# U's large loads ahead of its single rows, and the sine part of batch 0 ahead of the cosine part on TensorE

## The chip, the cores and the metric

The kernel runs on one core of a Trainium2 chip. The metric is the time of one execution on the device, in microseconds. The core's engines each work through their own queue in order: TensorE (PE, with its weight loads listed as PEld), VectorE (DVE), ScalarE (ACT), GpSimd (POOL) and SyncE (SP, which issues transfers only). Semaphores tie the queues together. SP and ACT can ask for transfers on a hardware queue, POOL on a software queue; all of them are served by the same 16 DMA engines.

## The reference

```python
X = np.fft.fft(x, axis=1)          # x: 8 x 3136 x 256
X = np.fft.fft(X, axis=2)
x = X.real
h = x.transpose(0, 2, 1) @ U @ V   # U: 3136 x 32, V: 32 x 3136
u = x + h.transpose(0, 2, 1)
out = u + np.maximum(u @ w_ch1, 0) @ w_ch2   # 256 -> 1024 -> 256
```

A Fourier transform over the sequence and over the channels (only the real part is kept), a low-rank mixing along the sequence, and a two-layer perceptron over the channels, with residual sums.

## The kernel before

The sequence transform is written as matrix products with tables of sines and cosines. These tables are made on the chip at the start: `phase` (L229) reduces the angle on DVE, `sine` (L235) and `cosine` (L241) apply the sine function on ACT (`cosine` takes an absolute value first, then a sine, with a tile `ab` between). `tabs[0]` holds sines, `tabs[1]` cosines, each with eight rows `i` of 393 columns and 32 further columns. Symmetries of the tables save work: `odd_row` makes a sine row in full, the other sine rows are made in half and mirrored (`mirror_even`), and most cosine rows are copies of sine rows, turned or with the sign changed (`cosine_odd`, `cosine_low`, `cosine_high`), spread over ACT, POOL and DVE.

The input is folded before it meets the tables. The sequence of a batch is cut into four quarters of 98 partitions with eight elements each, and one partition more for single rows; a "forward" quarter is added to or taken from a "reversed" one. U is folded so too, by `fold_u` (L262): sixteen float32 matmuls on PE with flip matrices `fl` and `nfl` (made by POOL and, in `signs`, L253, by DVE). `UR` holds U reversed, `UF` forward; each comes in one large load of 196 KB (L143) and one load of a single row (`load_0r`, L94 and `load_0f`, L88). `lower_u` copies one half of the result out of PSUM on ACT and `join_u` makes sum and difference on DVE.

Batch 0 has its own path, for it must be ready first. Four large loads (`first_r`, `first_f` for `a` = 0 and 1) and one load of the single rows (`first_0`) bring it into `xb` as bf16, on POOL's queue. `fold_pe(typ, t, a, first)` (L797) folds one quarter with four matmuls of 512 columns: `typ` 0 is the part that meets the sine table, 1 the part for the cosine table; `t` is 1 for the reversed load, 0 for the forward one; `a` is the half of the sequence. `M[typ, a]` are the PSUM tiles that it fills. `keep_m` copies M of `a` = 0 out of PSUM; `half_m` (L820) then makes the half sums and differences on DVE into `G[0]`, the stationary operand of `seq` (L437), the sequence transform.

The folded U is transformed by `transform_u` (L293) in four steps, `us[0]` to `us[3]` for sines and `uc` for cosines: `contract` (sixteen matmuls, L303), `keep` (ACT, L309), `turn` (eight matmuls, L316), and `evict` (ACT, L321 and L322), which fills the tables' 32 further columns. A value `hv` per partition halves some table rows (`halve`, L326) and is used in `evict`.

PE's clock is kept up with filler matmuls (`busy`, L170) whose results nobody reads.

Up to L964 the order of the program is the order on each engine (a manual schedule). After the start a loop over 49 chunks of 512 rows runs the perceptron on PE, with the folds and transforms of batches 1 to 7 spread between its steps by a table of due slots. Loads of later batches are issued by POOL when their buffers come free; SP issues the transposed copies of `u`, the output and the loads of single columns (L499, L508).

Of the kernel before, what the change touches and what calls it, by code (L numbers as in the profile page):

```python
# [8 lines left out]
TWO_PI = 2.0 * math.pi  # L9
HALF_PI = 0.5 * math.pi  # L10
BF16 = mybir.dt.bfloat16
FP32 = mybir.dt.float32
I32 = mybir.dt.int32
AL = mybir.AluOpType
AF = mybir.ActivationFunctionType
# [3 lines left out]
KP = PQ + 1  # L19
NI = 8  # L20
NQ = 393
# [6 lines left out]
def kernel(  # L28
# [9 lines left out]
    nc = tc.nc  # L38
    B, S, D = x.shape
    R = moe_U.shape[1]  # L40
# [9 lines left out]
    gen = setup.enter_context(tc.tile_pool(name="gen", bufs=2))  # L50
# [8 lines left out]
    def rev(t, b, a, w):  # L59

        return bass.AP(t.tensor, t.offset + (b * S + S - 784 - a * HALF) * w,
                       [[8 * w, PQ], [1, 8 * w]])
# [10 lines left out]
    def first_f(a):  # L73
        gather(xb[:PQ, a, 0].rearrange("p i d -> p (i d)"), x, S // 8 - 1,
               xidx[:PQ, 0, a:a + 1], 8 * D, D)

    def first_r(a):
        nc.gpsimd.dma_start(out=xb[:PQ, a, 1].rearrange("p i d -> p (i d)"), in_=rev(x, 0, a, D))

    def first_0():  # L80
        nc.gpsimd.dma_start(out=xb[PQ:KP].rearrange("p a t i d -> p a (t i) d"),
                            in_=bass.AP(x.tensor, x.offset,
                                        [[D, 1], [HALF * D, 2], [0, 2 * NI], [1, D]]))
# [4 lines left out]
    def load_0f(t, dst_f, b, w, q):  # L88
        lo = t.offset + b * S * w
        q.dma_start(out=dst_f[PQ:KP],  # L90
                    in_=bass.AP(t.tensor, lo + (NI - 1) * w,
                                [[w, 1], [HALF * w, 2], [-w, NI], [1, w]]))

    def load_0r(t, dst_r, b, w, q):  # L94
        lo = t.offset + b * S * w
        q.dma_start(out=dst_r[PQ:KP].rearrange("p a i d -> p a (i d)"),
                    in_=bass.AP(t.tensor, lo, [[w, 1], [HALF * w, 2], [1, NI * w]]))
# [17 lines left out]
    def const(v):  # L115
        t = cpool.tile([P, 1], FP32, name=f"c{len(consts)}", tag=f"c{len(consts)}")
        nc.vector.memset(t, v)
        consts.append(t)
        return t

    consts = []
    c_pi, c_npi, c_nhp = const(math.pi), const(-math.pi), const(-HALF_PI)
    c_half = {b: const(-float(2 ** (b - 1))) for b in (15, 17)}
    UF = gen.tile([KP, 2, NI, R], FP32, tag="uf", name="uf", bufs=1)
    UR = gen.tile([KP, 2, NI, R], FP32, tag="ur", name="ur", bufs=1)
    xidx = cpool.tile([P, B, 2], I32, name="xidx")
    krow = gen.tile([P, 2, NQ], FP32, tag="krow", name="krow", bufs=1)
    ncol = cpool.tile([P, NI], FP32, name="ncol")
# [8 lines left out]
    lrow = gen.tile([P, 2, P], FP32, tag="lrow", name="lrow", bufs=1)  # L137
    pcol = gen.tile([P, 1], FP32, tag="pcol", name="pcol", bufs=1)
    QD = P // 2
    load_0r(moe_U, UR, 0, R, nc.sync)  # L140
    load_0f(moe_U, UF, 0, R, nc.sync)
    for t, n0, step in ((UR, S - 784, -HALF), (UF, 1, HALF)):
        nc.sync.dma_start(out=t[:PQ].rearrange("p a i d -> p a (i d)"),  # L143
                          in_=bass.AP(moe_U.tensor, moe_U.offset + n0 * R,
                                      [[8 * R, PQ], [step * R, 2], [1, 8 * R]]))
    first_r(0)
    first_f(0)
    first_0()
    nc.gpsimd.iota(fl[:, 0], pattern=[[1, P]], base=-(PQ - 1), channel_multiplier=1,
                   allow_small_or_imprecise_dtypes=True)  # L150
    nc.gpsimd.iota(fl[:, 1], pattern=[[1, P]], base=0, channel_multiplier=-1,
# [18 lines left out]
    def busy(n, a=None):  # L170

        idle = psum.tile([P, 512], FP32, tag="p2", name="idle", bufs=2)
        for _ in range(n):
            if a is None:
                nc.tensor.matmul(idle[:, :256], ones[:, :P], ones[:], start=True, stop=True)
            else:
                nc.tensor.matmul(idle[:, :NQ], a[:PQ, 0, 0, :P], a[:PQ, 0, 0, :NQ],
                                 start=True, stop=True)

    busy(26)  # L180
    for t in (EOF_, EOR_):
        nc.vector.memset(t.rearrange("p a i d -> p (a i) d")[:, :, 257:258], 0.0)
    G = [[cpool.tile([KP, NI, GW], BF16, name=f"g{s}{par}", tag=f"g{s}{par}") for par in range(2)]
# [7 lines left out]
    def va_zeros(s):  # L191
# [6 lines left out]
    tabs = [cpool.tile([KP, NI, 2, QW], BF16, name="tabs", tag="tabs"),  # L198
            cpool.tile([KP, NI, 2, QW], BF16, name="tabc", tag="tabc")]
# [41 lines left out]
    def cosine(out_, y, bits):  # L241
        pp = y.shape[0]
        ab = gen.tile(list(y.shape), FP32, tag="ab", name="ab", bufs=1)
        nc.scalar.activation(ab[:], y, AF.Abs, bias=c_half[bits][:pp])
        nc.scalar.activation(out_, ab[:], AF.Sin, scale=TWO_PI / 2 ** bits, bias=c_nhp[:pp])

    NH = NQ // 2 + 1
    flip = cpool.tile([P, 2, P], BF16, name="flip")
    nid = gen.tile([P, P], BF16, name="nid", bufs=1)
    phe = gen.tile([KP, NI // 2, 2, NH], I32, name="phe", bufs=1)  # L250
    GU = gen.tile([KP, 2, 2, NI, R], BF16, tag="gu", name="gu", bufs=1)

    def signs():  # L253

        nc.vector.tensor_scalar(nfl[:], fl[:], 0.0, -1.0, op0=AL.is_equal, op1=AL.mult)
        nc.vector.tensor_single_scalar(fl[:], fl[:], 0.0, op=AL.is_equal)
        for t in (fl, nfl):
            nc.vector.tensor_copy(t[:KP, 0, PQ:KP], t[:KP, 1, PQ:KP])
        nc.scalar.copy(flip[:], fl[:])
        nc.scalar.copy(nid[:], nfl[:, 1])  # L260
# [19 lines left out]
    def join_u(ur):  # L280

        for typ, op in ((0, AL.subtract), (1, AL.add)):
            nc.vector.tensor_tensor(GU[:, typ], pf[0][:], ur[:], op=op)

    hv = cpool.tile([P, 1], FP32, name="hv")
    hw = cpool.tile([P, 1], FP32, name="hw")
# [43 lines left out]
    def cells(t, i, col, step, n, skew):  # L330

        v = tabs[t][:, i, :, :]
        return bass.AP(v.tensor, v.offset + col, [v.ap[0], [QW + skew, 2], [step, n]])

    def turned_copy(dst, src, sgn):

        if sgn > 0:
            nc.gpsimd.tensor_copy(dst, src)
        else:
            nc.scalar.activation(dst, src, AF.Copy, scale=-1.0)  # L340

    def mirror_even(t, i):

        odd_m = (i + 1) // 2 % 2 == 1
        dst, src = cells(t, i, 0, 1, NH - 1, 1), cells(t, i, NQ - 1, -1, NH - 1, 0)
        if i == 1:
            nc.scalar.copy(dst, src)
        else:
            turned_copy(dst, src, 1 if odd_m == (t == 0) else -1)

    def cosine_odd(i):

        dst, src = cells(1, i, 1, 1, NQ - 1, 0), cells(0, i, NQ - 2, -1, NQ - 1, 1)
        if i == 4:
            nc.gpsimd.tensor_copy(dst, src)
        else:
            nc.scalar.activation(dst, src, AF.Copy, scale=1.0 if i == 0 else -1.0)

    def cosine_low(i):

        dst, src = cells(1, i, NH - 1, 1, NH, 1), cells(0, i, NQ - 1, -1, NH, 0)
        if i == 1:
            nc.gpsimd.tensor_copy(dst, src)
        else:
            nc.vector.tensor_single_scalar(dst, src, -1.0, op=AL.mult)
# [385 lines left out]
    def odd_row(i):  # L751
        pho = gen.tile([KP, 2, NQ], I32, tag="pho", name="pho")
        phase(pho[:], krow[:KP], ncol[:KP, i:i + 1], 15)
        sine(tabs[0][:, i, :, :NQ], pho[:], 15, 1)
# [3 lines left out]
    cosine_odd(2)  # L758
    odd_row(4)
    signs()  # L760
    nc.vector.tensor_scalar(hv[:], ncol[:, NI - 1:NI], 0.0, -0.5, op0=AL.is_equal, op1=AL.mult)
    nc.vector.tensor_scalar(hw[:], ncol[:, NI - 1:NI], 0.249, -0.5, op0=AL.is_gt, op1=AL.mult)
    nc.vector.scalar_tensor_tensor(hv[:], hv[:], 1.0, hw[:], op0=AL.add, op1=AL.add)
    odd_row(6)
    pf = fold_u()
    busy(2)
    for m, i in enumerate((7, 5, 3, 1)):
# [9 lines left out]
        if i == 3:  # L777
            mirror_even(0, 3)
    join_u(ur)
    mirror_even(0, 1)  # L780
    cosine_low(1)
    cosine_odd(4)
# [9 lines left out]
    def gathered(typ, a, tags):  # L792

        M[typ, a] = [psum.tile([KP, 4, P], FP32, tag=t, name="m", bufs=2 if t == "p2" else 3)
                     for t in tags]

    def fold_pe(typ, t, a, first):  # L797

        for n in range(2):
            v = xb[:, a, t, 7 - 4 * n if t else 4 * n, :]  # L800
            for m, w in enumerate((-1, 1)):
                nc.tensor.matmul(M[typ, a][n][:],  # L802
                                 nid[:KP, :KP] if typ == 0 and (t + m) % 2 else flip[:KP, 1, :KP],
                                 bass.AP(v.tensor, v.offset + P, [v.ap[0], [-D if t else D, 4],
                                                                  [w, P]]),
                                 start=first and m == 0, stop=not first and m == 1)
# [34 lines left out]

    gathered(0, 0, ("p1", "p1"))
    gathered(1, 0, ("p1", "p2"))
    for t in (1, 0):
        for typ in range(2):
            fold_pe(typ, t, 0, t == 1)
    gathered(0, 1, ("p2", "dft"))
    fold_pe(0, 1, 1, True)
    cosine(tabs[1][:, 7, :, NH - 1:NQ], phe[:, 0], 15)
    us[0]()  # L850
# [1 line left out]
    for a in range(2):  # L852
        load_second(a)
    us[1]()
    cosine_odd(0)
    fold_pe(0, 0, 1, False)
    us[2]()
    for n in range(2):
        keep_m(0, n)
    phase(pd[:], lrow.rearrange("p a l -> p (a l)"), pcol[:], 17)  # L860
    gathered(1, 1, ("p1", "p1"))
    fold_pe(1, 1, 1, True)
    busy(3, tabs[0])
    for n in range(2):
        half_m(0, 0, n)
    us[3]()
# [1 line left out]
        half_m(0, 1, n)  # L868
    nc.vector.tensor_copy(cells(1, 7, 0, 1, NH - 1, 1), cells(1, 7, NQ - 1, -1, NH - 1, 0))
    halve(1)  # L870
    cosine(tabs[1][:, 3, :, NH - 1:NQ], phe[:, 2], 15)
    nc.scalar.copy(cells(1, 3, 0, 1, NH - 1, 1), cells(1, 3, NQ - 1, -1, NH - 1, 0))
    cosine_low(5)
    cosine_high(1)
# [131 lines left out]
```

## Time and profile before

| what | value |
|---|---|
| runs, median of 3 | 458.23 us (457.78 to 458.64) |
| the profiled execution, whole time | 459.67 us |
| its span, first to last instruction | 457.9 us |
| PE busy in the span | 445.5 us |
| ACT busy | 293.3 us |
| DVE busy | 348.6 us |
| mean granted PE clock | 0.992 |
| moved by DMA | 65.38 MB, mean 143 GB/s |

A row of the timeline gives the start in us from the span's start, the duration (of a merged group: from its first start to its last end), engine, line, operation, tiles as out<-in, shape, count, and in brackets how long the engine was idle before and what ended that. A matmul's own row is longer than its share of PE, because matmuls are pipelined; the distance between the starts of two neighbours is what one costs. A row of the chain of waits gives start, duration and what the chain went through.

### The profile page before, as it was taken

What the parts mean: (1) busy time and instruction counts of PE and PEld (TensorE: products, weight loads), DVE (VectorE), ACT (ScalarE), POOL (GpSimd) and SP (SyncE); (2) the same over time, 40 slices, a digit from 0 to 9 for tenths busy, and PEclk for the clock granted to TensorE, in tenths of its full rate; (3) what the DMA queues carried; (4) which work ended last, traced back from release to release, by engine and by line L of the source; (5) the groups of instructions that cost most, each with busy time, mean ns of one, the idle gap of its engine ahead of it and who ended that gap; (6) DMA issues with size and microseconds to landing.
All of it is one profiled execution on the core that took longest, in us unless ns stands there. A gap on an engine that the chain in (4) does not pass through costs nothing.

```text
span 457.9 us, 8080 instructions
## 1 busy us (share of the span) xinstructions
PE 445.5 (97%) x2991; PEld 323.1 (71%) x3044; DVE 348.6 (76%) x813; ACT 293.3 (64%) x563; POOL 63.2 (14%) x115
## 2 busy tenths in 40 slices
PE   7999999999999999999999999999999999999996
PEld 4555766666777777777777777777777777777775
DVE  8488999969897869977997779877898666443433
ACT  7476745756865577655865586656865586655562
POOL 8824212200012002100102002200000000000000
PEclk9799999999999999999999999999999999999999
DMA  6993997994378636683378527792253333334343
GB/s 133 219 225 62 174 204 165 157 205 112 114 214 210 138 89 158 195 220 109 84 219 201 146 73 191 208 209 71 69 111 97 93 97 88 94 115 108 102 129 103
DMA packets 103238, 65.38 MB, mean 143 GB/s; under 512 B 73794, under 2 KB 99612, under 8 KB 100452
## 3 DMA queue, kind: packets, MB, share of 16 engines
q1 hardware_dynamic: 97534, 39.10, 37.4%
q0 software_dynamic: 5664, 25.75, 20.9%
q8 instruction: 24, 0.39, 0.3%
q14 instruction: 16, 0.13, 0.1%
HBM read 29.33 MB, written 25.69 MB: 120 GB/s over the span
## 4 chain that ended last, share of the span: by engine, by line
PE 85%; DVE 7%; DMA 3%; issue 2%; SPq 1%; ACT 1%; POOL 0%; DVEq 0%; ACTq 0%
PE p L707 35%; PE p L691 32%; PE pt L452 5%; PE ph L665 4%; PE pth L428 2%; DMA uf<-in_moe_U_dram 2%; DMA cr<-in_x_dram 1%; PE m L802 1%; DVE eor L386 1%; PE pst L604 1%; PE pst L613 1%; SPq L508 1%; PE pf L268 1%; DVE eof L386 1%; DVE u L681 1%
## 5 line engine op out<-in xcount | busy, mean ns | idle before, releaser
L693 ACT ACTIVATE h<-p 128x512 bf16<-128x512 f32 x392 | 223.6, 598 | 129.5 <-PE p L691 116.9
L691 PE MATMUL p<-u,w 128*128 128x512 bf16 x734 | 208.6, 379 | 2.2 <-DVE u L681 0.5
L707 PE MATMUL p<-w,h 128*128 128x256 bf16 x1568 | 204.2, 273 | 1.3
L707 PEld LDWEIGHTS <-h 128*128 128x128 bf16 x1568 | 153.0, 98 | 51.4 <-DVE o L716 0.8
L691 PEld LDWEIGHTS <-w 128*128 128x128 bf16 x784 | 105.9, 144 | 35.5 <-issue 1.7
L713 DVE TENSOR_TENSOR o<-p,ut 128x4 f32<-128x4 f32 (+1 forms) x100 | 16.4, 164 | 56.8 <-PE p L707 54.4
L55 POOL DMA_INDIRECT xf<-in_x_dram,xidx x14 | 17.9, 1276 | 184.3 <-DVE eof L386 172.9
L716 DVE TENSOR_TENSOR o<-p,ut 128x254 f32<-128x254 f32 (+1 forms) x100 | 40.9, 409 | 0.0
L715 DVE TENSOR_TENSOR o<-p,ut 128x254 f32<-128x254 f32 (+1 forms) x100 | 40.8, 408 | 0.0
L681 DVE TENSOR_TENSOR u<-ph,S 128x512 bf16<-128x512 f32 (+23 forms) x63 | 34.5, 557 | 0.0
L681 DVE TENSOR_TENSOR u<-ph,T 128x512 bf16<-128x512 f32 (+23 forms) x63 | 34.4, 557 | 0.0
L386 DVE TENSOR_TENSOR eor<-xr 99x1024 bf16<-99x1024 f32 x28 | 34.1, 1220 | 0.1
L386 DVE TENSOR_TENSOR eof<-xf 99x1024 bf16<-99x1024 f32 x28 | 33.7, 1220 | 0.0
L665 PE MATMUL ph<-va,ta 128*128 128x512 bf16 (+15 forms) x124 | 28.6, 328 | 0.1
L452 PEld LDWEIGHTS <-g 98*128 98x128 bf16 (+1 forms) x152 | 14.6, 98 | 13.0 <-issue 0.7
L459 DVE TENSOR_TENSOR tab<-pt,ev 128x32 bf16<-128x32 f32 x32 | 6.1, 191 | 16.8 <-PE pt L452 16.0
L395 DVE TENSOR_TENSOR eos<-eof,eor 99x1024 bf16<-99x1024 bf16 (+1 forms) x28 | 18.8, 687 | 0.0
L615 DVE TENSOR_TENSOR S<-evd,pst 128x392 bf16<-128x392 f32 (+1 forms) x24 | 13.6, 566 | 6.5 <-PE pst L613 6.1
L452 PE MATMUL pt<-tabs,g 98*128 98x425 bf16 x80 | 17.7, 344 | 0.0
L399 DVE TENSOR_TENSOR g<-eos 99x2048 bf16<-99x2048 bf16 (+1 forms) x14 | 17.0, 1220 | 0.0
L452 PE MATMUL pt<-tabc,g 98*128 98x425 bf16 x72 | 15.5, 344 | 0.0
L665 PEld LDWEIGHTS <-ta 128*128 128x128 bf16 (+1 forms) x128 | 11.9, 98 | 3.1 <-ACT ta L636 0.6
(188 smaller groups left out, 363.2 us busy)
## 6 DMA issues: line engine op xcount, KB each, us to landing
out_dram<-o SPq DMA_DIRECT2D x48, 512.0 KB
xr<-in_x_dram POOLq DMA_DIRECT2D x14, 784.0 KB, 7.0
xb<-in_x_dram POOLq DMA_DIRECT2D x2, 392.0 KB, 7.6
ut<-u SPq DMA_TRANSPOSE x49
w<-in_moe_w_ch_dram POOLq DMA_DIRECT2D x1, 512.0 KB, 8.4
out_dram<-o SPq DMA_DIRECT2D x4, 128.0 KB
va<-in_moe_V_dram POOLq DMA_DIRECT2D x2, 196.0 KB, 5.8
w<-in_moe_w_ch_dram POOLq DMA_DIRECT2D x1, 256.0 KB, 6.7
```

The source lines that it names most:

```text
L55: nc.gpsimd.indirect_dma_start(out_, None, bass.AP(t.tensor, t.offset, [[w, rows], [1, w]]), bass.IndirectOffsetOnAxis(idx, 0), element_of ...
L386: pin(nc.vector.tensor_tensor(dst[:, a, :, part * P:(part + 1) * P].rearrange("p i (k t) -> p i k t", k=2), lo, hi, op=AL.subtract if part ...
L395: pin(nc.vector.tensor_tensor(EOS[:, a, :, cols], EOF_[:, a, :, cols], EOR_[:, a, ::-1][:, :, cols], op=op))
L399: pin(nc.vector.tensor_tensor(G[b % 2][par][:, :, cols], EOS[:, 0, :, cols], EOS[:, 1, :, cols], op=AL.add if par == 0 else AL.subtract))
L452: nc.tensor.matmul(pt[:], g[:kp(i), i, P * typ:P * (typ + 1)], tabs[typ][:kp(i), i, par, :], start=(n == 0), stop=(n == NI // 2 - 1))
L665: nc.tensor.matmul(ph, TA[b % 2][:k, s * P:(s + 1) * P], VA[b % 2][:k, lo:hi], start=start, stop=True)
L681: nc.vector.tensor_tensor(u[:, s, col:col + hi - lo], ph[:, col:col + hi - lo], src, op=AL.add)
L691: nc.tensor.matmul(p1[:], W1[:, s, j::JT], k["u"][:, s, :], start=(s == 0), stop=(s == 1))
L693: LAST[0] = nc.scalar.activation(k["h"][:, j, :], p1[:], AF.Relu)
L707: nc.tensor.matmul(p2[:, t % w, :], h[:, j, rs], W2[:, j, :], start=(j == 0), stop=(j == JT - 1))
L715: nc.vector.tensor_tensor(o[:, ts, 1:P], p2[:, :w, 1:P], ut[:, ts, 1:P], op=AL.add)
L716: nc.vector.tensor_tensor(o[:, ts, P + 1:D], p2[:, :w, P + 1:D], ut[:, tT, P - 1:0:-1], op=AL.add)
```

## The change

```diff
-    load_0r(moe_U, UR, 0, R, nc.sync)
-    load_0f(moe_U, UF, 0, R, nc.sync)
+    load_0f(moe_U, UF, 0, R, nc.scalar)
     for t, n0, step in ((UR, S - 784, -HALF), (UF, 1, HALF)):
         nc.sync.dma_start(out=t[:PQ].rearrange("p a i d -> p a (i d)"),
                           in_=bass.AP(moe_U.tensor, moe_U.offset + n0 * R,
                                       [[8 * R, PQ], [step * R, 2], [1, 8 * R]]))
+    load_0r(moe_U, UR, 0, R, nc.sync)
+    first_0()
     first_r(0)
     first_f(0)
-    first_0()
...
-    busy(26)
+    busy(27)
...
     signs()
-    nc.vector.tensor_scalar(hv[:], ncol[:, NI - 1:NI], 0.0, -0.5, op0=AL.is_equal, op1=AL.mult)
-    nc.vector.tensor_scalar(hw[:], ncol[:, NI - 1:NI], 0.249, -0.5, op0=AL.is_gt, op1=AL.mult)
-    nc.vector.scalar_tensor_tensor(hv[:], hv[:], 1.0, hw[:], op0=AL.add, op1=AL.add)
+    cosine_odd(0)
     odd_row(6)
...
     join_u(ur)
+    nc.vector.tensor_scalar(hv[:], ncol[:, NI - 1:NI], 0.0, -0.5, op0=AL.is_equal, op1=AL.mult)
+    nc.vector.tensor_scalar(hw[:], ncol[:, NI - 1:NI], 0.249, -0.5, op0=AL.is_gt, op1=AL.mult)
+    nc.vector.scalar_tensor_tensor(hv[:], hv[:], 1.0, hw[:], op0=AL.add, op1=AL.add)
...
-    for t in (1, 0):
-        for typ in range(2):
-            fold_pe(typ, t, 0, t == 1)
     gathered(0, 1, ("p2", "dft"))
+    fold_pe(0, 1, 0, True)
+    fold_pe(0, 0, 0, False)
+    fold_pe(1, 1, 0, True)
     fold_pe(0, 1, 1, True)
...
-    cosine_odd(0)
     fold_pe(0, 0, 1, False)
     us[2]()
+    fold_pe(1, 0, 0, False)
+    ab3 = gen.tile([KP, 2 * NH], FP32, tag="ab3", name="ab3", bufs=1)
+    nc.scalar.activation(ab3[:], phe[:, 2].rearrange("p a k -> p (a k)"), AF.Abs,
+                         bias=c_half[15][:KP])
...
-    busy(3, tabs[0])
+    busy(2, tabs[0])
...
-    cosine(tabs[1][:, 3, :, NH - 1:NQ], phe[:, 2], 15)
+    nc.scalar.activation(tabs[1][:, 3, :, NH - 1:NQ], ab3.rearrange("p (a k) -> p a k", a=2),
+                         AF.Sin, scale=TWO_PI / 2 ** 15, bias=c_nhp[:KP])
```

U's single row for `UF` is now asked for by ACT's queue, the two large loads of U come first on SP's, and `UR`'s single row last of the three. On POOL `first_0` is issued ahead of batch 0's large loads. Three small instructions for `hv` move behind `join_u` on DVE. `cosine_odd(0)` moves up on ACT to stand ahead of the fourth sine row. On PE the sine quarters of batch 0 come ahead of the cosine quarters: of the four quarters of `a` = 0 the last cosine one is put behind U's turn. The cosine of table row 3 is made in two places: the absolute value earlier, the sine where the whole was. One filler matmul is added at the start and one taken away later. What is computed stays the same.

## The prediction

> **What bounds the kernel now.** I read the page first, then the chain of waits over the first 26 us, the busy time by stretches of the clock, the timelines of the engines, and the DMA queues.
>
> ```profile
> PE 445.5 (97%) x2991; PEld 323.1 (71%) x3044; DVE 348.6 (76%) x813; ACT 293.3 (64%) x563; POOL 63.2 (14%) x115
> ```
>
> TensorE is busy in 97% of the span (page, part 1), so time is won only where it stands idle or runs at half clock; both happen in the first 17 us, where the diff works. The chain of waits there, with start, duration, and what it is:
>
> ```profile
> 2.78 8.10 DMA uf<-in_moe_U_dram
> 10.88 0.14 issue
> 11.01 3.71 PE pf L268 x8
> ...
> 21.87 1.89 DVE g L822 x3
> ```
>
> The start hangs on U: its second large load is asked for at 2.78 and lands at 10.88, then TensorE folds U (L268), folds batch 0 (L802), and waits for VectorE's first three half sums (L822). The stretches of the clock (columns: busy time of PE, PEld, DVE, ACT, POOL, granted clock, DMA share, GB/s):
>
> ```profile
> 6.65:10.06 3.41, 1.76 (x9) 1.22 (x8) 3.27 (x11) 2.28 (x5) 3.11 (x7) 1.00 1.00 225
> 10.06:13.48 3.42, 3.24 (x9) 1.84 (x8) 1.70 (x5) 3.39 (x8) 3.11 (x7) 0.50 1.00 193
> 13.48:16.89 3.41, 3.41 (x10) 1.89 (x10) 1.83 (x6) 1.78 (x5) 2.99 (x6) 0.50 1.08 202
> 98.81:102.22 3.41, 2.60 (x18) 1.91 (x18) 2.18 (x5) 1.87 (x5) 0.00 (x0) 1.00 1.26 94
> ```
>
> A stretch of 3.41 us in which PE was busy 1.76 us (52%) was followed by two at half clock; one at 2.60 us (76%) kept the clock. So the wait for U costs twice: idle time, and then half speed from 10.06 to 16.89. PE's timeline gives the prices:
>
> ```profile
> 1.35 5.58 PE L175 MATMUL idle<-ones 128*128 128x256 bf16 x26 [1.35 <-DVE ones L169]
> 8.57 1.51 PE L268 MATMUL pf<-ur,fl 99*99 99x256 f32 x6 [1.65 <-DMA ur<-in_moe_U_dram]
> 9.92 0.91 PE L268 MATMUL pf<-ur,nfl 99*99 99x256 f32 x2
> ...
> 20.34 0.85 PE L303 MATMUL pu<-tabs,gu 98*32 98x393 bf16 x16
> 21.13 0.42 PE L802 MATMUL m<-xb,flip 99*99 99x512 bf16 x1
> ...
> 22.04 0.83 PE L316 MATMUL put<-sel,wu 128*98 128x64 bf16 x8
> 22.70 1.05 PE L802 MATMUL m<-xb,flip 99*99 99x512 bf16 x4
> 23.81 0.67 PE L177 MATMUL idle<-tabs 98*128 98x393 bf16 x3
> 24.32 0.89 PE L452 MATMUL pt<-tabs,g 98*128 98x425 bf16 x4
> ```
>
> At full clock six matmuls of the U fold take 9.92 - 8.57 = 1.35, 0.225 each; at half clock 3.71 / 8 = 0.46. Four of batch 0's fold take 22.04 - 21.13 = 0.91, 0.23 each at full clock. The sine contraction of U (L303) takes 0.79, its turn (L316) 22.70 - 22.04 = 0.66, one wide filler (L177) (24.32 - 23.81) / 3 = 0.17.
>
> **U's loads.** SyncE's timeline, and the hardware DMA queue in the answer for 6 to 8 us (packets, MB, share of 16 engines):
>
> ```profile
> 0.75 0.80 SPq L96 DMA_DIRECT2D ur<-in_moe_U_dram  x1
> 1.61 0.65 SPq L90 DMA_DIRECT2D uf<-in_moe_U_dram  x1
> 2.31 0.43 SPq L143 DMA_DIRECT2D ur<-in_moe_U_dram  x1
> ```
>
> ```profile
> q1 hardware_dynamic: 321, 0.31, 48.2%
> ```
>
> The two large loads are 0.39 MB, and 0.31 MB of this queue moves only between 6 and 8 us, when batch 0's first large load has passed. Now the large loads go first, at 0.75 and about 1.6, 1.5 and 1.2 us earlier than at 2.31 and 2.78, while POOL issues the small row (L81) ahead, and so asks for the first large load of batch 0 later, by the 0.4 to 0.8 that such an issue takes in SP's rows. What U lands at isn't shown by this trace: the bounds are 8.57, as now, and 0.75 + 0.80 + 1.3 = 2.9 (its first issue, and 0.196 MB at 0.31 MB in 2 us). I take "before 6.9", since both are asked for before any of batch 0's bulk is on the engines. UR's single row now stands last of the three on SP, behind 2 x 196 KB, and the first matmul needs it; UF's goes from ACT's queue. That issue on ACT is not in the trace; SP's rows bound it at 0.4 to 0.8. ACT has cover for it:
>
> ```profile
> 3.18 0.95 ACT L238 ACTIVATE tabs<-pho,c 99x786 bf16<-99x786 int32 x1 [1.15 <-DVE pho L233]
> ...
> 5.46 0.86 ACT L357 ACTIVATE tabc<-tabs 99x784 bf16<-99x784 bf16 x1
> ...
> 8.79 0.95 ACT L238 ACTIVATE tabs<-pho,c 99x786 bf16<-99x786 int32 x1 [1.13 <-DVE pho L233]
> ...
> 14.06 0.52 ACT L347 COPY tabs<-tabs 99x392 bf16<-99x392 bf16 x1
> 16.15 0.62 ACT L244 ACTIVATE ab<-phe,c 99x394 f32<-99x394 int32 x1 [1.57 <-DVE gu L283]
> 16.81 0.62 ACT L245 ACTIVATE tabc<-ab,c 99x394 bf16<-99x394 f32 x1
> 21.32 0.49 ACT L309 CAST wu<-pu 128x393 bf16<-128x393 f32 x1 [3.89 <-PE pu L303]
> ```
>
> It idled 1.15 us before its first sine, so I take 0; without cover it costs up to 0.8 on ACT's chain.
>
> **U's fold.** With U there, it starts when the flip matrices are ready and the fillers end:
>
> ```profile
> 6.63 0.15 DVE L258 COPY nfl<-nfl 99x1 f32<-99x1 f32 x1
> 6.70 0.15 DVE L761 TENSOR_SCALAR hv<-ncol 128x1 f32<-128x1 f32 x1
> ```
>
> The matrices are ready at 6.78; 26 fillers end at 6.93, 27 at about 7.0 (0.1 for one more, since the clock is full by then). So the fold runs from 7.0, with no hole: stretch 6.65 to 10.06 is then over 95% busy and the clock stays. 16 x 0.225 = 3.60, to 10.60; two fillers 0.22, to 10.82; four quarters of batch 0 in 16 x 0.23 = 3.64, to 14.46.
>
> **ACT and DVE around it.** The three hv instructions leave DVE's path ahead of the fourth sine row: that is about 0.3 earlier (8.5 in place of 8.79). cosine_odd(0), 0.86 at L357, goes into ACT's gap, which shrinks to about 0.85: nothing. ACT's last table copy then ends at 14.58 - 0.3 = 14.28, just ahead of PE's 14.46. Next on ACT come Abs, Sin and the eviction: 14.28 + 0.62 + 0.62 + 0.49 = 16.0. The hv instructions come back behind U's join on DVE, which has waited there for PE until now: nothing. The Abs of table row 3 is only moved, into a gap on ACT.
>
> **The new order on PE.** L303 from 14.46 to 15.25; sine quarter of the other half 0.91, to 16.16; turn 0.66 (its input is there at 16.0), to 16.82; eight matmuls of the cosine part 1.82, to 18.64; two fillers 0.34, to 18.98. VectorE's three half sums, 1.89 from 16.2, end at 18.1 and are covered. The first real transform matmul, at 24.32 now, then starts at 18.98: 5.3 us earlier.
>
> **What the quarters need.** The last one of the sine part comes from POOL's fourth large load:
>
> ```profile
> 6.74 1.01 POOL L55 DMA_INDIRECT xb<-in_x_dram,xidx  x1 [0.30 <-issue]
> ```
>
> ```profile
> DMA to landing us min/median/max: 7.5/8.0/8.8
> ```
>
> The second fence is from the answer on the tile xb. The load lands at 6.74 + 8.8 = 15.5 at the latest; PE now wants it at 15.25. POOL's issue time does not change (three instructions change places), and the engines have U's 0.39 MB out of the way earlier. So 0 to 0.3 is lost; up to 1.1 if the first load's 0.8 carries through. I take 0.
>
> Behind 24 us I take it that all work follows PE; the one load of which the chain says otherwise is rival (3). So 459.67 - 5.3 = 454.4 for the profiled execution (the span and what lies around it); that execution stands 1.44 above the median, so 458.23 - 5.3 = **452.9** on the scale of the runs. Its own range: 452.2 to 453.8.
>
> **Rivals.** (1) **The clock drops anyway.** The stretch 10.06 to 13.48 was 95% busy, mostly with float32 matmuls, and did not bring the clock back; so these may not count. Then it drops at 10.06: 2.4 matmuls of U left at 0.46, fillers 0.44, four of batch 0's fold at 0.46 to 13.48, the other twelve at 0.23: 16.2 in place of 14.46, a gain of 3.6, so 454.6; 456.4 if it stays low until 16.89. Against it: the same rows also fit a threshold between 95 and 100%. [...]
>
> (2) **U lands no earlier**, because UR's row waits behind the large loads and batch 0's bulk: PE starts at 8.57 as now, the clock falls, and only the new order gains: L303 four matmuls earlier, at 20.34 - 0.91 = 19.43, then 0.79, 0.91, 0.66, 1.82 and 0.34 as above, to 23.95 in place of 24.32: 0.4, so 457.8. For it: 0.31 MB of U moved only once batch 0's first load had passed. Against it: the engines are empty when U is asked for.
>
> (3) **The gain is given back at the column loads.**
>
> ```profile
> 94.95 6.87 DMA cr<-in_x_dram
> ```
>
> This load ends a wait at 101.8, and the DMA engines are full there (share 1.26 in the stretch from 98.81); if it lands no earlier, all 5.3 are lost: 458.2. Against it: its queue's first issue follows the compute, so it moves too.
>
> (4) **Slower: the quarters come late and the clock falls again.** If the load above landed after 16.9, PE would idle over 1.65 us in the stretch 13.48 to 16.89, and drop to half clock for two stretches (3.4 lost) and a third one while it waits for evictions (1.7): 1.7 + 3.4 + 1.7 = 6.8, so 1.5 slower, 459.7. It needs the load to be 1.4 later than the latest landing above.
>
> **Numbers.** Forecast 0.66, rival (1) 0.17, (2) 0.07, (3) 0.05, (4) 0.05. A measurement can tell about 0.2%, 0.9 us: faster 0.83, same 0.12, slower 0.05. The range goes from 451.9 (own low end and 0.3 for a shorter fold) to 456.5 (both ends of rival (1)).
>
> **What would show it.** Right: L268 from about 7.0 with no DMA wait, granted clock 1.00 from 6.65 on, L303 near 14.5, the first L452 near 19, cr landing near 96.5. Wrong: a second stretch at 0.50, a DMA wait ahead of L268 or of a quarter, or an ACT chain that ends later than 14.6.

## The result, and the profile after

| | before | changed |
|---|---|---|
| median | 458.23 us (457.08 to 460.0, 7 runs) | 454.88 us (454.4 to 461.75, 7 runs) |
| ratio to before | | 0.9923, 95% interval 0.9902 to 0.9943 |
| profiled execution, span | 457.9 us | 453.4 us |
| mean granted clock in it | 0.992 | 0.999 |

By the medians the change makes the kernel 3.35 us faster; the ratio of the runs gives 0.77%. A few runs fall into a second, slower state (here the one at 461.75 us, at a granted clock of 0.992); the ratios, and the 74 runs of the kernel before that are sorted below, leave these out. The forecast was 452.9, a gain of 5.3; the measured time lies inside the stated range, towards its slow side.

TensorE's timeline of the changed kernel (its fold of batch 0 is now line 803):

```profile
1.35 4.96 PE L175 MATMUL idle<-ones 128*128 128x256 bf16 x27 [1.35 <-DVE ones L169]
6.55 1.51 PE L268 MATMUL pf<-ur,fl 99*99 99x256 f32 x6 [0.24 <-issue]
7.90 0.59 PE L268 MATMUL pf<-ur,nfl 99*99 99x256 f32 x2
8.33 1.46 PE L268 MATMUL pf<-uf,fl 99*99 99x256 f32 x6
...
13.46 0.42 PE L803 MATMUL m<-xb,nid 99*99 99x512 bf16 x1 [0.15 <-DMA xb<-in_x_dram]
...
14.46 0.85 PE L303 MATMUL pu<-tabs,gu 98*32 98x393 bf16 x16
15.62 0.38 PE L803 MATMUL m<-xb,flip 99*99 99x512 bf16 x1 [0.30 <-DMA xb<-in_x_dram,xidx]
...
18.91 0.50 PE L177 MATMUL idle<-tabs 98*128 98x393 bf16 x2
19.25 0.89 PE L452 MATMUL pt<-tabs,g 98*128 98x425 bf16 x4
```

U's fold starts at 6.55 in place of 8.57 and has no wait for a load; its second half follows the first at once. Two waits for batch 0's loads have come in their place, 0.15 and 0.30 us: a load wait ahead of a quarter is one of the signs that the prediction had named for being wrong. The first real transform matmul stands at 19.25 in place of 24.32, 5.07 earlier. The stretches of the clock, with the columns as before:

```profile
5.15:8.56 3.41, 3.17 (x21) 2.38 (x19) 3.10 (x9) 3.38 (x7) 3.09 (x6) 1.00 0.95 141
8.56:11.97 3.41, 3.31 (x17) 2.16 (x16) 3.31 (x9) 3.41 (x7) 2.92 (x7) 1.00 1.01 190
11.97:15.39 3.42, 3.19 (x27) 1.37 (x25) 3.24 (x12) 3.06 (x7) 3.36 (x8) 1.00 1.01 196
```

PE is busy in 93 to 97% of each and the clock stays at 1.00, where the profile of before had two stretches at 0.50. The chain of waits no longer goes through U:

```profile
6.64 8.94 DMA xb<-in_x_dram,xidx
15.57 0.04 issue
15.62 1.03 PE m L803 x4
```

It goes through the forward load of the second half of batch 0, asked for at 6.64 and landed at 15.57. Later in the chain the column load ends 4.98 us earlier than before, at 96.84:

```profile
90.43 6.41 DMA cr<-in_x_dram
```

and the last instruction of the chain, at 454.46 before, is at 449.49, 4.97 earlier:

```profile
454.46 0.20 DVE o L716
```

```profile
449.49 0.20 DVE o L716
```

(The first of these two rows is from the chain of before, the second from that of the changed kernel.) So of the 5.07 us at the start 4.97 arrive at the end of the computation, and 4.5 in the span: behind the last computation the span of before goes on for 3.24 us and that of the changed kernel for 3.7. SyncE's last four output issues take 3.48 us there, 3.17 before; why is not shown. But the medians show 3.35 only. That distance, and which part of the change did it, were the questions for the experiments.

### The profile page after: what moved, and what is told of

Its sections match the earlier page's. It is cut to its first block, busy times and chain, and to the rows that moved or that the text cites. A ratio compares the mean times of both kernels' runs of the same rounds, so it can differ in the third digit from the quotient of the medians.

```text
span 453.4 us, 8081 instructions
## 1 busy us (share of the span) xinstructions
PE 441.6 (97%) x2991; PEld 321.5 (71%) x3044; DVE 347.8 (77%) x813; ACT 293.2 (65%) x563; POOL 63.4 (14%) x115
## 4 chain that ended last, share of the span: by engine, by line
PE 84%; DVE 6%; DMA 3%; issue 2%; POOL 1%; ACT 1%; SPq 1%; DVEq 0%; ACTq 0%; POOLq 0%
PE p L707 35%; PE p L691 32%; PE pt L452 5%; PE ph L665 4%; PE pth L428 2%; DMA xb<-in_x_dram,xidx 2%; DMA cr<-in_x_dram 1%; DVE eor L386 1%; PE pst L604 1%; PE pst L613 1%; SPq L508 1%; PE m L803 1%; DVE eof L386 1%; DVE u L681 1%; DVE o L716 1%
## 5 line engine op out<-in xcount | busy, mean ns | idle before, releaser
L452 PEld LDWEIGHTS <-g 98*128 98x128 bf16 (+1 forms) x152 | 14.6, 98 | 13.0 <-issue 0.7
L452 PE MATMUL pt<-tabs,g 98*128 98x425 bf16 x80 | 17.7, 344 | 0.0
L452 PE MATMUL pt<-tabc,g 98*128 98x425 bf16 x72 | 15.5, 344 | 0.0
```

Of the source, the lines that this page charges most:

```text
L452: nc.tensor.matmul(pt[:], g[:kp(i), i, P * typ:P * (typ + 1)], tabs[typ][:kp(i), i, par, :], start=(n == 0), stop=(n == NI // 2 - 1))
```

## The experiments

Each ran on a chip beside runs of the kernel before; medians compare within one group of runs. The theory to be tested: U's early landing, with the idle time and the half clock that it saves, is the whole gain. The rivals: the new order on PE carries a share; and the profile of before shows a price that its median doesn't pay.

**The kernel before, once more** (no edit).

> The kernel before once more, unchanged, for the granted clock of each of its runs. Theory (clock's phase): the stretches of 3.41 us by which the clock is granted begin at another point in each run, so the wait for U costs two stretches of half clock in some runs (clock 0.992, as in the profile, about 459.5) and fewer in others (clock above 0.994, about 457.5); the median then stands some 1 us below the profiled execution, and a gain read from that execution is about 1 us too large on the scale of medians. Rival (the profile itself costs the difference): the clock is 0.992 in every run and the times differ without it.

Median 457.53 (12 runs). The clock differs from run to run as the theory says. The 74 runs of the kernel before in the three groups, sorted by granted clock:

| granted clock | runs | median | lowest to highest |
|---|---|---|---|
| 0.9975 to 1.0 | 33 | 456.59 us | 455.81 to 457.6 |
| 0.9945 to 0.9974 | 18 | 457.50 us | 456.81 to 459.16 |
| under 0.9945 | 23 | 459.54 us | 457.56 to 462.5 |

The profiled execution of before_again is one that kept its clock:

```profile
8.51 1.51 PE L268 MATMUL pf<-ur,fl 99*99 99x256 f32 x6 [1.52 <-DMA ur<-in_moe_U_dram]
...
11.23 1.51 PE L268 MATMUL pf<-uf,fl 99*99 99x256 f32 x6 [0.79 <-DMA uf<-in_moe_U_dram]
...
21.66 0.89 PE L452 MATMUL pt<-tabs,g 98*128 98x425 bf16 x4
```

```profile
6.77:10.18 3.41, 1.89 (x10) 1.25 (x8) 3.27 (x11) 2.44 (x6) 3.21 (x8) 1.00 1.00 223
10.18:13.59 3.41, 2.62 (x14) 1.80 (x13) 1.73 (x6) 3.38 (x7) 3.07 (x6) 1.00 1.00 194
```

(Timeline of PE, then the stretches.) The same two waits for U stand there, 1.52 and 0.79 us, but the stretch that begins at 6.77 was busy for 1.89 us, 55%, and the next one kept full clock. The first transform matmul comes at 21.66, not 24.32: the profile that the prediction was made from had paid 2.66 us for the clock. By the table, 23 of the 74 runs have a clock near that profile's 0.992, and 33 kept theirs.

**The transfer part alone.** On the kernel before:

```diff
-    load_0r(moe_U, UR, 0, R, nc.sync)
-    load_0f(moe_U, UF, 0, R, nc.sync)
+    load_0f(moe_U, UF, 0, R, nc.scalar)
...
+    load_0r(moe_U, UR, 0, R, nc.sync)
+    first_0()
     first_r(0)
     first_f(0)
-    first_0()
...
-    busy(26)
+    busy(27)
```

> Before, with the transfer part alone (U's large loads first, UF's row on ACT's queue, UR's row third, first_0 ahead, 27 fillers); PE, ACT and DVE keep their old order. Theory A (U's landing and the clock that is kept carry all of it): the fold of U starts at about 6.6, the clock stays, and the first L452 starts at 19.0 to 19.4, as in the changed kernel; 454.9 within 0.4. Theory B (the new order on PE carries a share, since the last sine quarter now waits for its load only): the first L452 at 20 or later, and at least 1 us slower than the changed kernel, 456 or more.

Median 453.55, ratio 0.9914 (0.9887 to 0.9941). The first transform matmul:

```profile
15.51 0.42 PE L802 MATMUL m<-xb,flip 99*99 99x512 bf16 x1
...
18.71 0.89 PE L452 MATMUL pt<-tabs,g 98*128 98x425 bf16 x4
```

It comes at 18.71, earlier than the 19.25 of the whole change, and the last quarter of the sine part (15.51) waits for no load. Of the two theories A holds, for the transfers alone bring all of the gain; both its numbers were too slow, by 0.3 us in the trace and by 1 in the median.

**The order alone.** The changed kernel with these lines as before:

```diff
-    load_0f(moe_U, UF, 0, R, nc.scalar)
+    load_0r(moe_U, UR, 0, R, nc.sync)
+    load_0f(moe_U, UF, 0, R, nc.sync)
...
-    load_0r(moe_U, UR, 0, R, nc.sync)
-    first_0()
     first_r(0)
     first_f(0)
+    first_0()
...
-    busy(27)
+    busy(26)
```

> The changed kernel with U's loads, first_0 and the fillers as before: the new order on PE, ACT and DVE alone. Theory A: the fold of U starts at 8.5 as before, half clock follows, and the first L452 comes 0.4 earlier than before, 23.9; 457.8 (0.4 under before). Theory B: 1 us or more under before, 457.2 or less.

Median 457.12 against 457.43 of before, ratio 0.9991 (0.9972 to 1.001): this doesn't decide between no gain and theory A's 0.4 us, and the interval, which reaches to 1.3 us, doesn't exclude theory B's 1 us. Its profile (first transform matmul at 21.65) settles something else.

```profile
21.65 0.89 PE L452 MATMUL pt<-tabs,g 98*128 98x425 bf16 x4
```

The stretches:

```profile
5.63:9.04 3.41, 1.64 (x11) 1.19 (x10) 3.10 (x10) 3.41 (x6) 3.09 (x6) 1.00 0.99 231
9.04:12.45 3.41, 3.41 (x10) 2.25 (x9) 2.10 (x7) 2.79 (x6) 2.92 (x7) 0.50 0.97 184
12.45:15.87 3.42, 3.42 (x18) 2.14 (x18) 2.06 (x6) 3.14 (x7) 2.60 (x7) 1.00 1.04 198
```

PE was busy for 1.64 us (48%) and lost the clock at 9.04. The next stretch held float32 matmuls of U's fold and nothing else:

```profile
8.21 2.04 PE L268 MATMUL pf<-ur,fl 99*99 99x256 f32 x6 [1.77 <-DVE pho L233]
10.04 1.06 PE L268 MATMUL pf<-ur,nfl 99*99 99x256 f32 x2
10.89 2.23 PE L268 MATMUL pf<-uf,fl 99*99 99x256 f32 x6
```

(The profile puts the wait of 1.77 us down to VectorE's table phase, L233. The changed kernel has the same order there and starts this fold at 6.55, before that instruction, which begins at 7.27 there; so it is U's load, late as before, that is waited for.) The stretch was full (3.41 us), and the clock, 0.50 in it, was 1.00 behind it. So float32 matmuls did count as work here; whether as much as others is taken up in the last section.

**first_0 behind the large loads again.** The changed kernel with

```diff
-    first_0()
     first_r(0)
     first_f(0)
+    first_0()
```

> The changed kernel with batch 0's single rows asked for behind its first two large loads again. Theory (the single row is what counts): first_0 lands behind the forward load of a=0, at about 11.4, PE's first quarter waits for it from 10.3, and part of that is taken up by the wait for the last quarter: first L452 0.5 to 0.8 later than 19.25, 455.5. Rival (POOL's issue sets when the large loads land): all four land 0.8 earlier, PE's waits of 0.15 and 0.30 for them go, 454.4.

Median 454.06, ratio 0.9924 (0.9901 to 0.9947): no different from the changed kernel. The trace shows the mechanism all the same:

```profile
10.17 0.38 PE L175 MATMUL idle<-ones 128*128 128x256 bf16 x2
11.59 0.39 PE L803 MATMUL m<-xb,nid 99*99 99x512 bf16 x1 [1.03 <-DMA xb<-in_x_dram]
```

PE's first quarter waits 1.03 us for the single row, as the theory had it; the waits for the later quarters go, and the first transform matmul is at 19.63, 0.38 late (0.5 to 0.8 expected). That is too little for these medians, and the 455.5 that the theory gave was missed.

**The change and its transfer part side by side.** Two kernels without further edit.

> The changed kernel once more, beside loads_again on one chip. Theory A (the loads carry all of the gain; with U early the new order on PE asks for the last sine quarter before it has landed and puts four more matmuls ahead of the first L452): 0.3 to 0.7 slower than loads_again. Rival (the order is worth something beside the loads): as fast or faster than loads_again.

> The transfer part alone once more: first L452 near 18.7, 3.5 to 4 us under before, granted clock 0.998 or more in all runs. Theory A: 0.3 to 0.7 faster than after_again. Rival: as slow or slower.

Medians 454.18 and 454.31, ratios 0.9922 and 0.9923: no difference, theory A's 0.3 to 0.7 for the order missed. The first transform matmul in the two profiles:

```profile
19.33 0.88 PE L452 MATMUL pt<-tabs,g 98*128 98x425 bf16 x4
```

```profile
18.70 0.89 PE L452 MATMUL pt<-tabs,g 98*128 98x425 bf16 x4
```

That is 0.6 us in favour of the transfers alone; the spread of either kernel's runs, over 1 us, hides it, or part of it is lost behind. What these runs show is that the order adds no gain to the loads that can be told from their spread.

**Fewer fillers.** The transfer part, and

```diff
     pf = fold_u()
-    busy(2)
...
     fold_pe(1, 1, 1, True)
-    busy(3, tabs[0])
```

> The transfer part alone, without the two fillers behind U's fold and the three ahead of the first real transform. Theory (the fillers wait for VectorE's third half sum, at 18.15, and then take 0.51; the transform itself needs the first two only, at 17.5): first L452 at 18.0 to 18.2, 0.5 to 0.7 faster than loads_again. Rival (the transform's PSUM bank is the one that VectorE's fourth half sum reads, so it waits to 18.8 anyway): no faster than loads_again.

Median 452.80, ratio 0.9902 (0.9866 to 0.9937).

```profile
15.76 0.38 PE L801 MATMUL m<-xb,flip 99*99 99x512 bf16 x1 [0.24 <-DMA xb<-in_x_dram,xidx]
...
18.18 0.89 PE L452 MATMUL pt<-tabs,g 98*128 98x425 bf16 x4
```

The first transform matmul comes at 18.18, 0.52 ahead of loads_again, as the theory said; the clock stays without the fillers, 0.999 on average in the profiled execution. The median moved by 1.5, more than that, so the kernel was run once more.

> The kernel of loads_nofill once more (transfer part alone, without the two and the three fillers), on the chip of loads_nofill2. Theory: 1 to 1.5 under the changed kernel, 452.8, first L452 at 18.0 to 18.3. Rival (the difference of loads_nofill was the spread of the runs): 454 or more.

Median 453.43, ratio 0.9908 (0.9874 to 0.9942), first transform matmul at 18.13: the place in the trace repeats, and the median lies between what was expected (452.8) and what the rival gave (454 or more). The difference shrinks to 0.8 us from the changed kernel's 454.18, which is of another group. The four fillers ahead of the narrow product went next, in the same group:

```diff
     seq(0, 1, 0, 1)
-    busy(4, tabs[0])
```

> loads_nofill without the four fillers ahead of the narrow product as well. Theory (that product waits for ACT's last eviction into the cosine table, which ends 0.3 us after PE comes free; the fillers take 0.76): L524 at 23.9 in place of 24.3, 0.4 faster than nofill_again, clock kept. Rival (the two low-rank products behind it wait for POOL's clearing of their tiles, done at 25.3): no faster.

Median 451.98, ratio 0.9891 (0.9857 to 0.9925). The narrow product starts at 23.60, in nofill_again at 24.25:

```profile
22.77 0.89 PE L452 MATMUL pt<-tabs,g 98*128 98x425 bf16 x4
23.60 0.91 PE L524 MATMUL ptc<-tabc,g 98*32 98x425 bf16 x16
```

That is 0.65, a little more than the 0.4 expected; the medians are 1.45 apart, more than the trace accounts for. The mean granted clock of the profiled execution is 1.000. It is the fastest version measured, 5.2 us under the 457.18 of before in its group, and it leaves PE's new order out. Its interval overlaps that of the changed kernel, so against that one the gain of some 2 us rests on the medians and on the trace, where the narrow product of the changed kernel starts at 25.37.

**Fillers in place of the wait.** The kernel before with

```diff
-    busy(26)
+    busy(41)
```

> Before with 41 fillers in place of 26, so that PE has work until U's first large load is there; U is as late as before. Theory (two prices: the wait itself, and half clock in those runs whose stretch of 3.41 us was busy under about 54%): granted clock 0.996 or more in all runs, none at 0.991 to 0.993, median 456.5, 0.5 to 1 under before, and most of the distance to the changed kernel (2.5) is left. Rival (half clock is the larger part of the wait's price): within 1 us of the changed kernel. Rival (fillers change nothing): as before, runs at 0.992 among them.

Median 456.40 against 457.37; of its 12 runs one is under 0.9945 in clock (none was expected), where 23 of the 74 runs of before are. The ratio, 1.0 (0.9964 to 1.0036), doesn't confirm a gain: three runs took 459 to 460.3 us with a clock of 0.996 or more, one of them at 1.0, and no trace shows what held these up. The profile does show what the fillers cover:

```profile
8.26 1.51 PE L268 MATMUL pf<-ur,fl 99*99 99x256 f32 x6 [0.42 <-DVE pho L231]
...
21.49 0.89 PE L452 MATMUL pt<-tabs,g 98*128 98x425 bf16 x4
```

U is still late, the first transform matmul is at 21.49, beside 21.66 in the run of before that kept its clock and 19.25 in the changed kernel. So two prices stand apart: half clock, for which the table of before gives 0.8 us in the median (457.35 for all 74 runs, 456.59 for those that kept it), and the wait itself, 2.2 (456.40 less 454.18, on one chip). The rival that half clock is the larger part falls. That fillers save the 0.8 is not shown.

**UF's single row on SP.** The changed kernel with

```diff
-    load_0f(moe_U, UF, 0, R, nc.scalar)
...
     load_0r(moe_U, UR, 0, R, nc.sync)
+    load_0f(moe_U, UF, 0, R, nc.sync)
```

> The changed kernel with UF's single row asked for by SP, last of U's four, in place of ACT's queue. Theory (ACT's 1.27 us for that issue lies in a gap of ACT, and the row is wanted at 8.3 only): the table load starts at 0.75 again, the first sine at 3.2, U's fold at 6.5 to 6.9 and the first L452 at 19.2 to 19.4 as in the changed kernel; 454.2 within 0.4. Rival (on SP the row lands behind batch 0's bulk and the second half of U's fold waits for it): L268 waits for a load after 8.3, and 1 us or more is lost.

Median 454.45, ratio 0.9928 (0.99 to 0.9956), U's fold at 6.68, the first transform matmul at 19.50: the same within the runs. ACT's rows show what that issue costs there, first the changed kernel, then row_on_sp:

```profile
0.75 1.27 ACTq L90 DMA_DIRECT2D uf<-in_moe_U_dram  x1
2.04 1.28 ACT L238 ACT_TABLE_LOAD   x1 [2.04 <-issue]
3.34 0.95 ACT L238 ACTIVATE tabs<-pho,c 99x786 bf16<-99x786 int32 x1
```

```profile
0.75 1.28 ACT L238 ACT_TABLE_LOAD   x1 [0.75 <-PEq L995]
3.18 0.96 ACT L238 ACTIVATE tabs<-pho,c 99x786 bf16<-99x786 int32 x1 [1.15 <-DVE pho L233]
```

The issue takes 1.27 us and pushes the table load back from 0.75 to 2.04, but the first sine by 0.16 only.

## Why the prediction was right, and by how much it was off

- **U's landing** ("I take 'before 6.9'"): right. L268 waits for no load.
- **U's fold from 7.0 at full clock**: right, but 0.45 earlier than said. It starts at 6.55 and keeps 0.225 us a matmul, (7.90 - 6.55) / 6. The start differs with the clock of the run: the 27 fillers took 4.96 us here and were done at 6.31; in after_again they took 5.66, and the fold starts at 6.85.
- **ACT's issue at 0, covered**: right in its effect, though the issue took 1.27 us where SP's rows gave 0.4 to 0.8 as bounds.
- **L303 at 14.46, the first L452 at 18.98**: 14.46 and 19.25. That the first of these is met to the hundredth is luck: the fold of U began 0.45 early, and the four quarters behind it took 4.18 us (10.28 to 14.46) in place of 3.64, with the wait of 0.15 for a load and a hole ahead of 11.63 for which the profile gives no cause. Behind it, the last 0.27 is a term that was taken as 0: the wait for the fourth large load, 0.30. It landed at 15.57, and the latest that the rows of before allowed was 15.5, so U's earlier transfer freed nothing for it. The step "the engines have U's 0.39 MB out of the way earlier" failed there.
- **"all work follows PE"**: right to 0.1 us up to the last computation; the output behind it gave back 0.5. The column load came 4.98 earlier, so rival (3) didn't happen.
- **458.23 - 5.3 on the scale of the runs**: this is the mis-sized step. The 1.44 us by which the profiled execution stands above the median were carried over as a constant. They are no constant: that execution had lost its clock for two stretches, and before_again, whose stretches begin 0.12 us later (6.77 in place of 6.65; busy for 1.89 us in place of 1.76), had not. Worked from runs that kept their clock, the gain in the trace is 21.66 - 19.25 = 2.4, and the medians agree: 456.59 less 454.18 is 2.4 (the first from three groups, the second from one of them). The lost clock adds 0.8 us in the median of before (457.35 for the 74 runs), so the change is worth some 3.2, near the 3.35 measured. The forecast's own range ended at 453.8; that the measured time lies inside the stated one is luck, for its slow end was set for rival (1), the loss of the clock in the changed kernel, and not for this.
- **Rival (1)**, that float32 matmuls don't count for the clock: fallen, by order_only, where a stretch of nothing else (9.04 to 12.45, 3.41 us busy) brought it from 0.50 to 1.00. The prediction's answer to it, that the rows also fit a threshold between 95 and 100%, doesn't hold either: in loads_again a stretch that was busy for 2.73 us (80%), with fillers, raised the clock. At the start of these kernels the clock fell after stretches that were busy for 48% (order_only) and 52% (before), and stayed after one of 55% (before_again).
- **Rival (2)** and **rival (4)** didn't happen. The new order, which (2) priced at 0.4, shows no gain clear of noise, with U late or early.

The stretches begin at another point in each of these runs: full clock begins at 5.15 us in the changed kernel's profile (a filler costs 0.21 us up to there and 0.11 behind it), at 6.65 in that of before and at 6.77 in before_again.

## What to carry to other kernels

Before a gain is read from one profile, ask what in that execution depends on chance: here the wait for U, which left TensorE busy for 52% of a stretch in one execution and 55% in another, was paid in half clock in the first and not in the second, and the median showed only a part of that price, 0.8 us. Put the large loads that end the first wait at the head of their queue, ahead of the single rows: U's fold then began at 6.55 in place of 8.57. The transfer part was the whole gain here, as far as these runs can tell, and the gain stayed when POOL's order (first0_back, 454.06) or ACT's issue (row_on_sp, 454.45) was taken out of it; so the order on SP's queue is what is left as its cause, though no run had that alone. When a wait is gone, look again at the fillers that were put in for it: without nine of them the narrow product starts 1.2 us earlier (23.60; 24.83 in loads_again).

## What was not expected of the hardware

The busy share of a stretch doesn't settle by itself what the clock does next. These stretches of 3.41 us are from the traces; "float32" stands for U's fold:

| run | stretch | PE busy, mostly with | clock in the stretch | clock after it |
|---|---|---|---|---|
| order_only | 5.63 to 9.04 | 1.64 us, fillers and float32 | full | half |
| before | 6.65 to 10.06 | 1.76 us, float32 | full | half |
| before_again | 6.77 to 10.18 | 1.89 us, float32 | full | full |
| loads_only | 446.40 to 449.82 | 1.33 us, bf16 | full | half |
| before_filled | 448.90 to 452.31 | 1.46 us, bf16 | full | full |
| order_only | 449.36 to 452.77 | 1.73 us, bf16 | full | full |
| before | 10.06 to 13.48 | 3.24 us, float32 | half | half |
| order_only | 9.04 to 12.45 | 3.41 us, float32 | half | full |
| loads_again | 0.66 to 4.08 | 2.73 us, fillers (bf16) | half | full |

(In the last row half clock is read from the fillers, 0.21 us each up to 4.08 and 0.11 behind it, 27 of them in 4.44 us. The mean granted clocks of the executions in the three rows for the end of the kernel fit them: 0.998 in loads_only, 1.000 in before_filled, 0.996 in order_only.) At the end of the kernel 1.46 us of bf16 matmuls were enough to keep the clock, and at its start 1.76 us, mostly of float32, were not; to win it back, 2.73 us of fillers were enough and 3.24 us of float32 were not. Float32 matmuls that count for less than their time would fit all nine rows; no run tests this.

And the same small load (L90) took 0.65 us to issue on SP in before and 1.27 on ACT in the changed kernel.
